# A planned kernel whose order is now the best of six schedules, with two buffers for v and r and one for S

## The chip, the core and the metric

The kernel runs on one core of a Trainium2 chip. The core has five engines that run side by side, each with its own queue of instructions that it takes strictly in order: PE (TensorE, matmuls), DVE (VectorE), ACT (ScalarE), POOL (GpSimd) and SP (SyncE, which here issues nearly all DMAs). [...] The metric is the device time of one execution in microseconds (us), as the median of several runs; less is better.

## The reference

Three stages follow each other. The first is a recurrence over 768 time steps for 4 batches x 8 heads with a 40x40 state each; the second and third are feed-forward blocks on 3072 tokens of width 320.

```python
for t in range(S):                                   # S = 768, state: (4, 8, 40, 40)
    y[:, :, t] = np.einsum('bhd,bhde->bhe', rt, state)
    Sa = np.einsum('bhde,bhe->bhd', state, at)
    state_decay = state * wt[:, :, None, :] - np.einsum('bhd,bhe->bhde', Sa, bt)
    state = state_decay + np.einsum('bhd,bhe->bhde', vt, kt)
...
h = x @ w_in                                         # 320 -> 2048, "Moe1"
g = h * np.tanh(np.log1p(np.exp(np.minimum(h, 20.0))))   # h itself where h > 20
x = g @ w_out                                        # 2048 -> 320
...
gate = 1.0 / (1.0 + np.exp(-(x @ w_gate)))           # 320 -> 1536, "Moe2"
return (gate * (x @ w_val)) @ w_out                  # 1536 -> 320
```

## The kernel before

**The recurrence ("attention").** The 768 steps are cut into 12 windows of 64. In a window each of the 4 batches is a unit, so there are 48 units; two units make a pair. For a unit, `load` brings `PA` (decays and a) and `KB` (k and b), `load2` brings `R` and `V` (r and v), `scale` forms decay products on DVE, `natural` (PE L441) transposes k and b. For a pair, `gram` (PE L423) forms the products of k, b and a. For a window, `solve` inverts a triangular system: 30 short DVE steps (`stmp`, L41, and `X`, L46, by turns) on 16x16 blocks, a round trip through DRAM, and for each of the two pairs four PE products (L564, L572, L581, L592/593). Then per unit or pair: `rv` (PE L459, r times v, reads `R` and `V`), `proj` (PE L622, r times the state `S` that the same batch had a window earlier; it reads `R` and `S`), `rhs` (PE L642 and L648), `zed` (PE L673), `close` (PE L706, then DVE L710), and `state` (PE L739, a transpose of the new state, which ACT copies to `S` at L743). `proj` is the last reader of its unit's `R`.

**The feed-forward blocks.** Moe1 takes a window's 256 tokens as soon as its four units are closed: 16 PE products into `ph` (L933, 8 matmuls of 128x256 each), ACT and DVE for the nonlinearity in groups of four (Sigmoid L976, Arctan L984, Sin L987, and a product on DVE, L41), a split in a high and a low part (`hi`, `lo`), and PE products into `x` (L1010 to L1023; L1007 opens a window's accumulation). Moe2 (PE L933 into `pgv`, L1137 to L1139) starts when all of the attention and nearly all of Moe1 are done, since its weights take over the attention's memory. Weights arrive as 64-bit numbers and are decoded on the core by DVE instructions in fours (L784, L786, L788, L794): Moe1's at the start, Moe2's ("parked" in DRAM) through the whole first part.

**What sets the order.** No order is written by hand. Every operation is recorded in a `Plan` with its engine (or a choice of engines), its planned duration, what it reads and writes, and a priority (`prio`, an early or late due time that its caller computes from constants such as `L` and `LA`). `Plan.order` then simulates the engines: step by step it takes, of the operations that could start within a few hundredths of a microsecond, the one of smallest priority, and so fixes for each engine the order in which its instructions are issued. On PE a rule beside the priorities steers the mix of attention and feed-forward products (`ratio`, `debt`, `DENSE`). The planned durations of DVE and ACT operations get `EACH` on top (0.08 and 0.09 us).

**Buffers.** `Attention.RINGS` gives the number of buffers of each kind of tile. A tile may be written when every reader of the tile that had its buffer before is done; the planner counts with that (`alloc`), and the semaphores of the built program enforce it. `R` and `V` have one buffer each: the DMAs of the next unit's r and v wait for the `proj` of the unit before.

Of the kernel before, what the change touches and what calls it, by code (L numbers as in the profile page):

```python
# [15 lines left out]
B, H, S, D = 4, 8, 768, 40  # L16
# [39 lines left out]
SEM = {('PE', 'PE'): 0.0, ('PE', 'DVE'): .32, ('PE', 'Act'): .32, ('Act', 'PE'): .37, ('DVE', 'PE'): .37, ('Pool', 'PE'): .37, ('SP', None): 0.0}  # L56
# [4 lines left out]
WAIT, URGENT = .09, 60.0  # L61
TICK, WARM = 3.413, 3060
TABLE = 1.283
EACH = {'DVE': .08, 'Act': .09}
SWITCH = .16
BIAS = {'PE': 0.0, 'DVE': 0.0, 'Act': 0.0, 'Pool': 0.0, 'SP': 0.0}
WIN = {'PE': .06, 'DVE': .06, 'Act': .06, 'Pool': .06, 'SP': .06}


class Op:  # L70
    __slots__ = ('eng', 'dur', 'lat', 'fn', 'alloc', 'prio', 'kind', 'need', 'out', 'ready', 'end', 'tiles', 'id', 'port')


class Plan:
# [7 lines left out]
    def __init__(s, rings, now=False):  # L82
        s.rings, s.now = rings, now
        s.ops, s.last, s.reads, s.users = [], {}, {}, {}
        s.n = 0

    def op(s, eng, dur, r, w, fn, alloc=(), prio=0.0, kind=None, lat=0.0, port=True):
        if s.now:
# [3 lines left out]
        if isinstance(eng, dict):  # L92
            eng = {e: d + EACH.get(e, 0.0) for e, d in eng.items()}
        elif eng in EACH:
            dur += EACH[eng]
        o.eng, o.dur, o.lat, o.fn, o.alloc, o.prio, o.kind = eng, dur, lat, fn, alloc, prio, kind
# [25 lines left out]
        return s.n  # L122

    def order(s, ratio):
        free = {}
        ready = {}

        def release(o):
            for e in o.eng if isinstance(o.eng, dict) else (o.eng,):
                ready.setdefault(e, []).append(o)  # L130

        for o in s.ops:
            for d in o.need:
                d.out.append(o)
            o.need = len(o.need)
            if not o.need:
                release(o)
        rings = {t: [None] * n for t, n in s.rings.items()}
        count = {t: 0 for t in rings}
        done, past, fetched = [], [], []  # L140
        debt = dma = acc = 0.0
        tick = 0
        warm = False
        table = last = None
        att = sum(o.kind == 'att' for o in s.ops)

        ports = {}

        def port(o, e):
            return ports.get('Pool' if e == 'DVE' else 'DVE', 0.0) if o.port and e in ('DVE', 'Pool') else 0.0  # L150

        def start(o, e):
            t = max(free.get(e, 0.0), port(o, e))
            if e == 'Act' and o.kind and o.kind != table:
                t += TABLE
            t = max(o.ready, t)
            if o.kind == 'bulk':
                t = max(t, dma - BACK)
            if o.kind == 'fetch' and len(fetched) >= 8:
                t = max(t, fetched[-8])  # L160
            if isinstance(o.eng, dict):
                b = BIAS if att else {}
                end = t + o.eng[e] + b.get(e, 0.0)
                if any(max(o.ready, free.get(x, 0.0), port(o, x)) + d + b.get(x, 0.0) < end for x, d in o.eng.items() if x != e):
                    return None
            used = {}
            for k in o.alloc:
                c = count[k[0]] + used.get(k[0], 0)
                used[k[0]] = used.get(k[0], 0) + 1
                old = rings[k[0]][c % len(rings[k[0]])]  # L170
                for u in s.users.get(old, ()):
                    if u.end is None:
                        return None
                    t = max(t, u.end + SEM.get((u.eng, e), .27))
            return t

        while len(done) < len(s.ops):
            best = None
            for e, l in ready.items():
                c = [(t, o) for t, o in ((start(o, e), o) for o in l) if t is not None]  # L180
                if not c:
                    continue
                m = min(t for t, o in c)
                late = [(o.prio, o.id, t, o) for t, o in c if m + WIN.get(e, 0.0) < t <= m + (FIRST if o.kind == 'first' else WAIT)]
                c = [(o.prio, o.id, t, o) for t, o in c if t <= m + WIN.get(e, 0.0)]
                if late and e != 'PE':
                    top = min(late, key=lambda x: x[:2])
                    if top[0] + URGENT < min(c, key=lambda x: x[:2])[0]:
                        c = [top]
                if e == 'PE' and ratio:  # L190
                    want = 'moe' if debt < 0 else 'att'
                    while past and past[0][0] < m - TICK:
                        past.pop(0)
                    if sum(x for _, x in past) < DENSE:
                        want = 'moe'
                    p = [x for x in c if x[3].kind == want]
                    c = p or c
                p = min(c, key=lambda x: x[:2])
                if best is None or p[2] < best[0]:
                    best = p[2], p[3], e  # L200
            assert best, "no operation can go next"
            t, o, e = best
            if isinstance(o.eng, dict):
                for x in o.eng:
                    ready[x].remove(o)
                o.dur, o.fn = o.eng[e], lambda f=o.fn, e=e: f(e)
                o.eng = e
            else:
                ready[e].remove(o)
            for k in o.alloc:  # L210
                g = rings[k[0]]
                g[count[k[0]] % len(g)] = k
                count[k[0]] += 1
            if e == 'SP':
                x = t
                for issue, kb in o.dur:
                    x += issue
                    dma = max(x + .65, dma) + kb / 360
                free['SP'], o.end = x, dma
            elif o.kind == 'fetch':  # L220
                free[e] = t + .1
                dma = max(t + 1.5, dma) + o.dur / 360
                o.end = dma + .8
                fetched.append(o.end)
            elif e == 'PE':
                x, left, work = t + (SWITCH if last and o.kind != last else 0.0), o.dur, o.lat or 2400 * o.dur
                last = o.kind
                while tick < int(x / TICK):
                    warm, acc, tick = acc >= WARM, 0.0, tick + 1
                while left > 1e-9:  # L230
                    rate = 1.0 if warm else .5
                    d = min(left / rate, (tick + 1) * TICK - x)
                    acc += work * d * rate / o.dur
                    left -= d * rate
                    x += d
                    if left > 1e-9:
                        warm, acc, tick = acc >= WARM, 0.0, tick + 1
                past.append((x, work))
                free['PE'] = o.end = x
                debt += o.dur if o.kind == 'moe' else -ratio * o.dur  # L240
                debt = max(-3.0, min(3.0, debt))
                if o.kind != 'moe':
                    att -= 1
            else:
                o.end = t + o.dur + o.lat
                if e is not None:
                    free[e] = t + o.dur
                if o.port and e in ('DVE', 'Pool'):
                    ports[e] = t + o.dur
                if e == 'Act' and o.kind:  # L250
                    table = o.kind
            done.append((t, len(done), o))
            for d in o.out:
                d.need -= 1
                d.ready = max(d.ready, o.end + (.32 if isinstance(d.eng, dict) else SEM.get((o.eng, d.eng), .27)))
                if not d.need:
                    release(d)
        s.span = max(o.end for o in s.ops)
        s.trace = done
        return [o.fn for _, _, o in done]  # L260


class Attention:
# [10 lines left out]

    RINGS = {'bk': 3, 'PA': 8, 'KB': 3, 'R': 1, 'V': 1, 'Kn': 6, 'E': 1, 'P64': 8, 'Gk': 3, 'Gb': 1, 'GS': 1, 'X': 1, 'U': 1, 'XT': 2, 'Q': 1,
             'stmp': 1, 'rs': 2, 'S': 2, 'xo': 1, 'vz': 2, 'gd': 2, 'xd': 2}

    def __init__(s, nc, plan, pool, dpool, banks, ins):  # L280
        s.nc, s.plan, s.p, s.dp, s.banks = nc, plan, pool, dpool, banks
# [20 lines left out]
    def tile(s, shape, tag):  # L302
        return s.p.tile(shape, F32, name=tag, tag=tag, bufs=s.RINGS[tag])

# [769 lines left out]
class Moe2:  # L1074
# [26 lines left out]
    def block(s, w, src, need, dst, at, then=lambda: None):  # L1101
# [51 lines left out]
        for f in range(NF2 + lag):  # L1153
# [16 lines left out]
RINGS = {**Attention.RINGS, 'hs': 2, 'tmp': 2, 'hi': 2, 'lo': 2, 'X6': 1, 'raw': 1, 'X7': 2, 'ph': 3, 'px': 1, 'dw': 1, 'dx': 1, 'raw2': 2,  # L1170
         'pgv': 3, 'g2': 2, 'g2h': 3, 'g2l': 3, 'y': 1}
# [292 lines left out]
```

## Time and profile before

| what | value |
|---|---|
| median of 3 runs | 1297.1 us (1292.1 to 1299.68) |
| the profiled execution | 1298.93 us, its span 1297.2 us |
| PE busy | 1159.2 us, 89% of the span |
| DVE busy | 860.7 us, 66% |
| ACT busy | 578.7 us, 45% |
| mean granted clock of PE | 0.94 |

The profile is of one execution. Its span runs from the first to the last instruction; what lies outside is 1.7 us. Busy times are sums over an engine's instructions without overlaps. [...] In a list of waits a row names the waiting engine and line, and behind the arrow what came last of that for which it waited.

### The profile page before, as it was taken

To read this page: it belongs to the slowest core of one execution; us is meant where nothing else is said; L and a number is where in the kernel's file an instruction comes from. 1 tells how busy PE (TensorE), PEld (TensorE's weight loads), DVE (VectorE), ACT (ScalarE), POOL (GpSimd) and SP (SyncE) were. 2 spreads that over 40 slices of the span, in tenths; PEclk is the share of its full clock that TensorE was granted. 3 is DMA by queue.
4 is the path that set the end of the run, shared out by engine and by line. 5 is a ranking of instruction groups with operands and counts; after the bars stand their busy time and mean duration, and the time that the engine had idled before them with its cause. 6 is when DMAs were issued, how large, how long until landed. Compare 5 with 4: busy or idle time off the path is not lost. (4 is left out here: it accounts for less than half of the span.)

```text
span 1297.2 us, 43316 instructions
## 1 busy us (share of the span) xinstructions
PE 1159.2 (89%) x18540; PEld 1093.2 (84%) x18540; DVE 860.7 (66%) x2238; ACT 578.7 (45%) x1061; POOL 126.4 (10%) x188
## 2 busy tenths in 40 slices
PE   4277759989999999988989798989999999999997
PEld 4266648888988888978878797989999999999997
DVE  7878888858787777768777677765844444444443
ACT  3134535656766576846547374774211111111111
POOL 2010110111011101010112100122100000000000
PEclk9997658989999899989979698989999999999999
DMA  8545463445353536445444434349500000000000
GB/s 242 150 133 135 101 173 86 123 111 134 102 143 97 152 98 154 101 97 142 119 116 124 120 85 112 80 111 369 166 24 23 23 24 23 24 24 11 11 11 14
DMA packets 205388, 132.47 MB, mean 102 GB/s; under 512 B 113537, under 2 KB 183554, under 8 KB 204802
## 3 DMA queue, kind: packets, MB, share of 16 engines
q1 hardware_dynamic: 196882, 117.80, 34.6%
q0 software_dynamic: 8304, 11.80, 3.8%
q8 instruction: 148, 2.42, 0.8%
q14 instruction: 54, 0.44, 0.1%
HBM read 98.08 MB, written 31.46 MB: 100 GB/s over the span
## 5 line engine op out<-in xcount | busy, mean ns | idle before, releaser
L933 PE MATMUL pgv<-X,w2in 128*128 128x256 f32 x2304 | 295.8, 281 | 0.0
L933 PEld LDWEIGHTS pgv<-X,w2in 128*128 128x128 f32 x2304 | 286.3, 188 | 0.0
L933 PE MATMUL ph<-X,win 128*128 128x256 f32 x1536 | 222.2, 295 | 5.9 <-ACT tmp L976 3.3
L933 PEld LDWEIGHTS ph<-X,win 128*128 128x128 f32 x1536 | 202.3, 199 | 10.9 <-ACT tmp L976 3.5
L1116 ACT ACTIVATE g<-pgv 128x256 f32<-128x256 f32 x144 | 55.4, 385 | 316.6 <-PE pgv L933 315.3
L1119 DVE TENSOR_TENSOR g<-pgv,g 128x256 f32<-128x256 f32 x144 | 60.9, 424 | 187.0 <-ACT g L1116 187.0
L1010 PE MATMUL x<-hi,wout 128*128 128x256 f32 x384 | 110.2, 308 | 6.6 <-DVE hi L51 4.0
L1011 PE MATMUL x<-hi,wout 128*128 128x256 f32 x384 | 103.5, 290 | 0.0
L1020 PE MATMUL x<-lo,wout 128*128 128x256 f32 x384 | 86.2, 307 | 0.7 <-DVE lo L46 0.7
L1010 PEld LDWEIGHTS x<-hi,wout 128*128 128x128 f32 x384 | 75.9, 198 | 11.8 <-DVE hi L51 4.3
L459 PE MATMUL at<-R,V 40*64 40x64 f32 x768 | 39.9, 255 | 43.2 <-DMA V<-vt 40.6
L1011 PEld LDWEIGHTS x<-hi,wout 128*128 128x128 f32 x384 | 76.3, 199 | 0.6
L459 PEld LDWEIGHTS at<-R,V 40*64 40x64 f32 x768 | 34.0, 164 | 49.8 <-issue 19.8
L41 DVE TENSOR_TENSOR hs<-hs,tmp 128x1024 f32<-128x1024 f32 x48 | 58.2, 1219 | 18.7 <-ACT tmp L987 18.5
L976 ACT ACTIVATE tmp<-ph 128x512 f32<-128x512 f32 x96 | 56.3, 597 | 30.4 <-PE ph L933 27.9
L1020 PEld LDWEIGHTS x<-lo,wout 128*128 128x128 f32 x384 | 61.1, 197 | 5.3 <-DVE lo L46 0.9
L46 DVE TENSOR_TENSOR g2l<-g,g2h 128x256 fp32r<-128x256 f32 x139 | 58.8, 424 | 4.0 <-ACT g2h L53 0.2
L466 DVE TENSOR_TENSOR VZ<-at,cst 64x256 f32<-64x256 f32 x96 | 40.3, 419 | 26.5 <-PE at L459 25.7
L987 ACT ACT_TABLE_LOAD x44 | 56.5, 1283 | 0.7
L976 ACT ACT_TABLE_LOAD x44 | 56.5, 1283 | 0.6
L46 DVE TENSOR_TENSOR lo<-hs,hi 128x512 fp32r<-128x512 f32 x82 | 54.7, 684 | 2.6 <-ACT hi L53 2.1
L987 ACT ACTIVATE tmp<-tmp,half 128x1024 f32<-128x1024 f32 x48 | 54.9, 1150 | 0.5
(177 smaller groups left out, 2389.8 us busy)
## 6 DMA issues: line engine op xcount, KB each, us to landing
PA<-pa SPq DMA_DIRECT2D x48, 260.0 KB
KB<-kb SPq DMA_DIRECT2D x48, 256.0 KB
dw<-w2in SPq DMA_DIRECT2D x30, 256.0 KB
w2in<-wd POOLq DMA_DIRECT2D x12, 640.0 KB, 14.7
R<-rt SPq DMA_DIRECT2D x48, 128.0 KB
V<-vt SPq DMA_DIRECT2D x48, 128.0 KB
gd<-Gb SPq DMA_DIRECT2D x48, 128.0 KB
wd<-dx SPq DMA_DIRECT2D x24, 256.0 KB
```

The source lines that it names most:

```text
L41: (nc.vector if e == 'DVE' else nc.gpsimd).tensor_tensor(out=out, in0=x, in1=y, op=ALU.mult)
L46: (nc.vector if e == 'DVE' else nc.gpsimd).tensor_tensor(out=out, in0=y, in1=x, op=ALU.subtract)
L459: nc.tensor.matmul(ps[64 * q:64 * q + 64, x:x + 64], d['V'][r, p, :], d['R'][r, p, :], start=True, stop=True)
L466: nc.vector.tensor_tensor(out=out, in0=ps[r, 0:256].rearrange("p (r a t) -> p r a t", r=2, a=2), in1=m, op=ALU.mult)
L933: nc.tensor.matmul(ps, W[:, a, c:c + 128], X[:, b, :], start=(i == 0), stop=(i == len(pairs) - 1))
L976: nc.scalar.activation(st['q', f // 4][:, f % 4 - 1:f % 4 + 1], st['ph', f // 2], AF.Sigmoid, scale=-1.0)
L987: nc.scalar.activation(st['q', g], st['q', g], AF.Sin, scale=-2.0, bias=s.half)
L1010: nc.tensor.matmul(p, O[:, 128 * j:128 * j + 128], hi, start=False, stop=False)
L1011: nc.tensor.matmul(p, O[:, 384 + 128 * j:512 + 128 * j], hi, start=False, stop=False)
L1020: nc.tensor.matmul(s.px[0][:, 256 * j:256 * j + 256], O[:, 128 * j:128 * j + 128], lo, start=False, stop=z and j == 1)
L1116: nc.scalar.activation(st['g', f], st['p', f][:, 0], AF.Sigmoid)
L1119: nc.vector.tensor_tensor(out=st['g', f], in0=st['p', f][:, 1], in1=st['g', f], op=ALU.mult)
```

## The change

`Plan.order` no longer schedules once. It makes six schedules. The first uses the callers' priorities and the PE rule as before. After each, `latest` walks the schedule backwards and computes for every operation the latest time at which it may start without lengthening that schedule (through its readers, the next operation on its engine, and the next user of its buffer); this time plus half of the caller's priority is the operation's priority in the next schedule. From the second on the PE rule is off (`ratio` 0). The schedule with the shortest planned span is kept. `EACH` is empty now, so planned durations of DVE and ACT are those written at each operation. `R` and `V` get two buffers each, `S` one instead of two. No operation is added or removed; where an operation has a choice of engines (DVE, ACT or POOL), the new schedule may choose otherwise.

```diff
@@ -61,14 +61,15 @@
-EACH = {'DVE': .08, 'Act': .09}
+PASSES, MIXED, PULL = 6, 1, 0.5
+EACH = {}
...
     def order(s, ratio):
+
+        best = None
+        for o in s.ops:
+            o.pred, o.list, o.aim = frozenset(o.need), o.eng, o.prio
+        for i in range(PASSES):
+            got = s.schedule(ratio if i < MIXED else 0)
+            s.log.append(s.span)
+            if best is None or s.span < best[0]:
+                best = s.span, [(t, k, o, o.eng) for t, k, o in got]
+            if i < PASSES - 1:
+                s.latest(got)
...
+    def latest(s, got):
+
+        late = {o: s.span - (o.end - t) for t, _, o in got}
...
+        for t, _, o in reversed(got):
+            x = late[o]
+            for d, lag in after[o]:
+                x = min(x, late[d] - (min(at[d] - t, o.took) if lag is None else o.end - t + lag))
+            late[o] = x
+        for o in s.ops:
+            o.prio = late[o] + PULL * o.aim
+
+    def schedule(s, ratio):
...
-    RINGS = {'bk': 3, 'PA': 8, 'KB': 3, 'R': 1, 'V': 1, 'Kn': 6, 'E': 1, 'P64': 8, 'Gk': 3, 'Gb': 1, 'GS': 1, 'X': 1, 'U': 1, 'XT': 2, 'Q': 1,
-             'stmp': 1, 'rs': 2, 'S': 2, 'xo': 1, 'vz': 2, 'gd': 2, 'xd': 2}
+    RINGS = {'bk': 3, 'PA': 8, 'KB': 3, 'R': 2, 'V': 2, 'Kn': 6, 'E': 1, 'P64': 8, 'Gk': 3, 'Gb': 1, 'GS': 1, 'X': 1, 'U': 1, 'XT': 2, 'Q': 1,
+             'stmp': 1, 'rs': 2, 'S': 1, 'xo': 1, 'vz': 2, 'gd': 2, 'xd': 2}
```

The diff puts 50 lines ahead of the attention's code, so what is L459 before is L509 in the changed kernel.

On PE, in the tenth window (units 36 to 39, batches 0 to 3), before: two closes (L706), two transposes of k and b (L441), the states of units 34 and 35 (L739), `proj` (L622) of unit 38, `rv` (L459) of unit 38, and the start of `gram` (L423).

```order
L706 MATMUL at_104<-VZ_113,Kn 40x104 x8
L706 MATMUL at_102<-VZ_113,Kn 40x104 x8
L441 MATMUL at_103<-cst,KB 128x104 x4
L441 MATMUL at_104<-cst,KB 128x104 x4
L739 MATMUL at_102<-cst,SU_110 40x40 x8
L739 MATMUL at_103<-cst,SU_111 40x40 x8
L622 MATMUL at_104<-R,S 40x64 x8
L459 MATMUL at_102<-R,V 64x64 x8
L423 MATMUL at_103<-PA,KB 64x64
```

The `rv` of unit 39 (the next L459) stands behind the rest of that gram alone, and its `R` and `V` may be loaded only after the L622 shown. In the changed kernel, the same place: a close's last transpose, Moe1 products, then both `rv` at once.

```order
L491 MATMUL at_103<-cst,KB 128x104 x4
L1070 MATMUL x_0_130<-lo,wout 128x256 x2
L1071 MATMUL x_1_131<-lo,wout 64x256
L1073 MATMUL x_1_131<-hi,wout 128x256
L983 MATMUL ph<-X_9790,win 128x256 x24
L509 MATMUL at_104<-R,V 64x64 x8
L509 MATMUL at_102<-R,V 64x64 x8
L983 MATMUL ph<-X_9790,win 128x256 x8
L789 MATMUL at_103<-cst,SU_110 40x40 x8
L1057 MATMUL x_0_130<-hi,zero 128x512
```

The `rv` of units 38 and 39 (L509) now stand side by side ahead of the `proj` (L672) of either, with a Moe1 product (L983) and a state (L789) behind them; the `proj` of units 38 and 39 come later, with a gram and Moe1 work between.

On DVE, in the first window's solve, before: the steps (`stmp`, `X`) follow each other with one `Gk` ahead.

```order
L46 TENSOR_TENSOR X<-X,stmp 128x8x8
L41 TENSOR_TENSOR stmp<-X,GS 128x63
L46 TENSOR_TENSOR X<-X,stmp 128x9x7
L41 TENSOR_TENSOR stmp<-X,GS 128x60
L46 TENSOR_TENSOR X<-X,stmp 128x10x6
L41 TENSOR_TENSOR stmp<-X,GS 128x55
L46 TENSOR_TENSOR X<-X,stmp 128x11x5
L41 TENSOR_TENSOR stmp<-X,GS 128x48
L46 TENSOR_TENSOR X<-X,stmp 128x12x4
```

In the changed kernel, the same steps, by turns with the decoding of Moe1's first weights (`hs`, `hi`, L836 to L844).

```order
L41 TENSOR_TENSOR stmp<-X,GS 128x63
L836 SCALAR_TENSOR_TENSOR hs<-hs 128x256
L46 TENSOR_TENSOR X<-X,stmp 128x9x7
L476 TENSOR_TENSOR Gk<-at_103,cst 128x512
L41 TENSOR_TENSOR stmp<-X,GS 128x60
L838 SCALAR_TENSOR_TENSOR hi<-hi 128x256
L46 TENSOR_TENSOR X<-X,stmp 128x10x6
L838 SCALAR_TENSOR_TENSOR hs<-hs 128x256
L41 TENSOR_TENSOR stmp<-X,GS 128x55
L844 SCALAR_TENSOR_TENSOR hi<-hi 128x256
L46 TENSOR_TENSOR X<-X,stmp 128x11x5
L844 SCALAR_TENSOR_TENSOR hs<-hs 128x256
```

So the decoding moved from behind the first solve into it.

## Rows read from the trace of the kernel before

**Rows 1.** A table by stage; busy time and count of each engine, granted clock, DMA share, GB/s

```profile
core 0: us, PE busy (x) PEld busy (x) DVE busy (x) ACT busy (x) POOL busy (x), PEclk, DMA share, GB/s
0.00:53.00 53.00, 18.88 (x376) 16.29 (x376) 40.67 (x122) 12.50 (x32) 7.07 (x17) 1.00 0.76 203
53.00:198.00 145.00, 96.47 (x2306) 85.31 (x2308) 120.34 (x383) 58.82 (x132) 15.18 (x25) 0.77 0.51 135
198.00:251.00 53.00, 51.88 (x1000) 47.20 (x997) 44.73 (x118) 32.97 (x62) 7.92 (x12) 0.96 0.42 110
251.00:871.00 620.00, 573.39 (x11547) 526.62 (x11547) 453.03 (x1139) 389.58 (x645) 77.97 (x113) 0.93 0.45 115
871.00:897.00 26.00, 25.32 (x212) 25.07 (x211) 13.29 (x22) 17.94 (x23) 12.72 (x16) 1.00 1.49 347
897.00:1297.00 400.00, 393.29 (x3113) 392.76 (x3112) 188.62 (x458) 66.91 (x171) 5.53 (x6) 1.00 0.14 41
```

**Rows 2.** L1007, which opens each Moe1 window's accumulation: least, median and longest ns, first and last start

```profile
L1007 PE MATMUL x<-hi,zero x12: 395/493/795, 198.5 to 871.0; 128*128 128x512 f32 x12
```

**Rows 3.** PE's waits, 251 to 871 us: total, times, longest

```profile
PE at L459 <- DMA V<-vt: 28.0, 15, 3.8
```

**Rows 4.** PE's waits, 53 to 198 us

```profile
PE at L564 <- DVE GS L558: 23.3, 2, 14.3
PE at L459 <- DMA V<-vt: 5.5, 3, 2.9
```

**Rows 5.** PE in order of time, units 38 and 39: start, duration, instructions, idle before

```profile
652.24 0.50 PE L739 MATMUL at<-cst,SU 40*40 40x40 f32 x16 [0.33 <-ACT S L743]
652.54 0.65 PE L622 MATMUL at<-R,S 40*40 40x64 f32 x16
652.99 0.93 PE L459 MATMUL at<-R,V 40*64 40x64 f32 x16
653.65 1.98 PE L423 MATMUL at<-PA,KB 40*64 40x64 f32 x64
658.52 0.98 PE L459 MATMUL at<-R,V 40*64 40x64 f32 x13 [2.88 <-DMA V<-vt]
```

**Rows 6.** The chain that ended last, at the same place: start, duration

```profile
653.95 0.36 SPq L351
...
654.35 4.04 DMA V<-vt
```

**Rows 7.** A stretch with such a wait (columns as in Rows 1)

```profile
650.00:660.00 10.00, 6.20 (x170) 5.62 (x171) 6.76 (x23) 2.56 (x7) 2.49 (x4) 0.66 0.54 130
```

**Rows 8.** PE in order of time: 13 Moe1 products back to back

```profile
858.49 12.63 PE L933 MATMUL ph<-X,win 128*128 128x256 f32 x104
```

**Rows 9.** DVE in order of time: two decodings side by side

```profile
46.48 0.42 DVE L786 SCALAR_TENSOR_TENSOR tmp<-tmp 128x256 int32<-128x256 int32 x1
46.81 0.42 DVE L788 SCALAR_TENSOR_TENSOR hs<-hs 128x256 int32<-128x256 int32 x1
```

**Rows 10.** Groups by line and form: operations that change engines, S, Sin and its table

```profile
L41 DVE TENSOR_TENSOR KB<-KB,E 128x512 f32<-128x512 f32 x29 | 21.8, 752 | 5.2 <-DMA KB<-kb 5.2
L51 DVE COPY hs<-ph 128x512 f32<-128x512 f32 x39 | 26.9, 690 | 33.4 <-ACT tmp L976 24.4 <-PE ph L933 8.4
L51 DVE CAST hi<-hs 128x1024 fp32r<-128x1024 f32 x22 | 15.2, 693 | 0.4
L743 ACT ACTIVATE S<-at 104x160 f32<-104x160 f32 x44 | 13.3, 302 | 13.4 <-PE at L739 12.4 <-DVE X L46 0.6
L987 ACT ACTIVATE tmp<-tmp,half 128x1024 f32<-128x1024 f32 x48 | 54.9, 1150 | 0.5
L987 ACT ACT_TABLE_LOAD x44 | 56.5, 1283 | 0.7
```

More of the change, by code (lines that the diff above doesn't have):

```diff
@@ L70 @@
 class Op:
-    __slots__ = ('eng', 'dur', 'lat', 'fn', 'alloc', 'prio', 'kind', 'need', 'out', 'ready', 'end', 'tiles', 'id', 'port')
+    __slots__ = ('eng', 'dur', 'lat', 'fn', 'alloc', 'prio', 'kind', 'need', 'out', 'ready', 'end', 'tiles', 'id', 'port', 'pred', 'list', 'aim', 'took')
 class Plan:
@@ L85, in __init__ @@
         s.n = 0
+        s.log = []
     def op(s, eng, dur, r, w, fn, alloc=(), prio=0.0, kind=None, lat=0.0, port=True):
@@ L124, in order @@
     def order(s, ratio):
+        best = None
[8 more added lines that the diff above has]
+                s.latest(got)
+        s.span = best[0]
+        for _, _, o, e in best[1]:
+            o.eng = e
+        s.trace = [x[:3] for x in best[1]]
+        return [(lambda f=o.fn, e=e: f(e)) if isinstance(o.list, dict) else o.fn for _, _, o, e in best[1]]
+    def latest(s, got):
+        late = {o: s.span - (o.end - t) for t, _, o in got}
+        after, rings, count = {}, {t: [None] * n for t, n in s.rings.items()}, {t: 0 for t in s.rings}
+        last = {}
+        for t, _, o in got:
+            a = after[o] = []
+            for d in o.pred:
+                after[d].append((o, SEM.get((d.eng, o.eng), .27)))
+            if o.eng is not None and o.eng in last:
+                after[last[o.eng]].append((o, None))
+            last[o.eng] = o
+            for k in o.alloc:
+                g, c = rings[k[0]], count[k[0]]
+                for u in s.users.get(g[c % len(g)], ()):
+                    if u is not o:
+                        after[u].append((o, SEM.get((u.eng, o.eng), .27)))
+                g[c % len(g)] = k
+                count[k[0]] = c + 1
+        at = {o: t for t, _, o in got}
+        for t, _, o in reversed(got):
[6 more added lines that the diff above has]
+    def schedule(s, ratio):
         free = {}
@@ L132, in order @@
         for o in s.ops:
-            for d in o.need:
+            o.eng, o.out, o.ready, o.end = o.list, [], 0.0, None
+            o.need = len(o.pred)
+        for o in s.ops:
+            for d in o.pred:
                 d.out.append(o)
-            o.need = len(o.need)
             if not o.need:
@@ L205, in order @@
                     ready[x].remove(o)
-                o.dur, o.fn = o.eng[e], lambda f=o.fn, e=e: f(e)
+                o.dur = o.eng[e]
                 o.eng = e
@@ L251, in order @@
                     table = o.kind
+            o.took = free.get(e, t) - t if e is not None else 0.0
             done.append((t, len(done), o))
@@ L258, in order @@
         s.span = max(o.end for o in s.ops)
-        s.trace = done
-        return [o.fn for _, _, o in done]
+        return done
 class Attention:
-    RINGS = {'bk': 3, 'PA': 8, 'KB': 3, 'R': 1, 'V': 1, 'Kn': 6, 'E': 1, 'P64': 8, 'Gk': 3, 'Gb': 1, 'GS': 1, 'X': 1, 'U': 1, 'XT': 2, 'Q': 1,
-             'stmp': 1, 'rs': 2, 'S': 2, 'xo': 1, 'vz': 2, 'gd': 2, 'xd': 2}
+    RINGS = {'bk': 3, 'PA': 8, 'KB': 3, 'R': 2, 'V': 2, 'Kn': 6, 'E': 1, 'P64': 8, 'Gk': 3, 'Gb': 1, 'GS': 1, 'X': 1, 'U': 1, 'XT': 2, 'Q': 1,
+             'stmp': 1, 'rs': 2, 'S': 1, 'xo': 1, 'vz': 2, 'gd': 2, 'xd': 2}
     def __init__(s, nc, plan, pool, dpool, banks, ins):
```

## The prediction, made before the changed kernel ran

> **What bounds the kernel now.** I read the table by stage first [rows 1]. The reader is to see where PE stands still. From 897 us to the end PE is busy 393 of 400 us at full clock: Moe2, a wall of matmuls whose order the change leaves as it is; the hand-over to it (871 to 897 us) has PE busy 25.3 of 26 us. From 251 to 871 us (attention and Moe1 mixed) PE is busy 573.4 of 620 us, so 46.6 us are idle, and the granted clock is 0.93 instead of 1.00, which costs at most 573.4 x 0.07 = 40 us more. From 53 to 198 us PE is busy only 96.5 of 145 us at clock 0.77, and DVE is the busiest engine, 120.3 us or 83%: that stage waits for the solves and for weights that DVE decodes. Before it (0 to 53 us) PE waits mostly for the first window's data and solve, 18.9 of 53 us busy; behind it (198 to 251 us) PE is full, 51.9 of 53. The last start of L1007, at 871.0 [rows 2], ends the mixed part. Everything before it that shortens PE's path shortens the kernel one for one, since PE does the same work afterwards.
>
> Then I read who keeps PE waiting. In the mixed part one cause stands out: `rv` waits for the DMA of `V`, 15 times, 28.0 us, so 60% of the 46.6 us idle [rows 3]. In the stage before, the largest is the solve (23.3 us), and `V` is 5.5 us [rows 4].
>
> **Part 1: two buffers for R and V.** One place shows the mechanism. `proj` of unit 38 (L622) starts at 652.54; only when it has read `R` may the next `R` be issued, at 653.95, then `V` at 654.35, which takes 4.04 us to land [rows 5, 6]. PE has only a gram (1.98 us) to put between, and stands idle 2.88 us before the next `rv`. From the L622's start to that L459's it is 6.0 us. With two buffers the transfer waits for the `proj` of two units earlier, and the new order puts both `rv` of a pair side by side, ahead of both `proj`. Between the releasing `proj` and the `rv` that needs the transfer now stand Moe1 products, states and a gram. I weighed the rows of the order with durations from the steady part (a Moe1 product of 8 matmuls is 12.63/13 = 0.97 us [rows 8], and so on by line). This estimate gives a median of 3.8 us of work between the two before, and 19 us with a least of 5.5 us now. The need is the 6.0 us from start to start less the 0.65 us of `proj`, so about 5.3 us. All 15 waits should go: -28.0 us, with a bound of 0 on the other side if something else is late at the same place. Next late there would be the states and `rhs`; the row with 0.33 us behind `ACT S` [rows 5] is the size I expect.
>
> **Part 2: the clock.** The wait stands in a stretch of 10 us with PE busy 6.2 us and clock 0.66 [rows 7]. The mixed part loses up to 40 us to the clock [rows 1]. If the loss follows the idle time, 60% of it, 24 us, belongs to the `V` waits. But these stretches also hold small attention matmuls, which stay. I take 20 us given back, with bounds 0 and 40.
>
> [...]
>
> **Part 3: one buffer for S.** `S` of a unit may be written when the `proj` of the one before has read it, and each `proj` waits for its own `S`, so 44 trips PE, ACT, PE become serial. The copy takes 0.302 us [rows 10]; a state that follows another waits 0.33 us for it [rows 5]. By the same weighing the new order has a median of 2.2 us of PE work between a state and its `proj` (7.3 before), a least of 0.8. That mostly covers it. I take +3 us; the bounds are 0 and 44 x 1.2 = 53 (half of a table load and a Sin, 1.283 + 1.150 [rows 10], that ACT may have to finish first).
>
> **Part 4: the order at the start.** Counted over the new order, 167 instead of 124 decoding instructions (L784 to L794) stand ahead of the eighth L710 on DVE, which closes the second window. Neighbours start 0.33 us apart though each shows 0.42 us [rows 9], so 43 of them are 14 us of DVE. With DVE at 83% the second window closes up to 17 us later. In exchange the last decoding of Moe1's weights comes after 470 instead of 510 DVE instructions, and the first L1007 stands ahead of 13 attention products that preceded it. I expect PE to lose time until the second window closes and to regain it when Moe1 is dense earlier: 0, with bounds -10 and +17.
>
> **Part 5: planned times without a margin, other engines.** The two neighbours in [rows 9] also show that `EACH` counted 0.08 us too much per DVE operation: 0.33 is the planned 0.34. The new plan has DVE about right. The choices move 17 products on `KB` from POOL to DVE (17 x 0.752 = +12.8 us), 25 copies of `hs` away from DVE (-17.3) and 11 casts of `hi` to it (+7.6) [rows 10]: +3 us on DVE, which is 73% busy in the mixed part [rows 1], hidden by PE. ACT gets two more pairs of table loads, 5 us, also hidden: it is 63% busy there. If PE's idle time shrinks, DVE comes to some 78%, still no bound. A denser plan without margins makes new small waits; PE's idle time beside `V` is 46.6 - 28.0 = 18.6 us. I take +5; the bounds are 0 and 18.6 (as much again).
>
> **The sum.** The profiled execution took 1298.9 us (span 1297.2 and 1.7 around it). 1298.9 - 28 - 20 + 3 + 0 + 5 = 1258.9. It lay 1.8 us above the median of 1297.1, so the forecast for the median is 1257 us.
>
> **Rivals.**
> A. The whole cold clock comes back with the waits: -28 - 40 + 3 = -65, so 1232. For it: wait and low clock stand together [rows 5, 7]. Against: from 53 to 198 us the clock is 0.77 although `V` costs only 5.5 us there [rows 1, 4], so small attention products lower it too.
> B. The start slips and stays late: +17 on the main sum, 1274. For it: DVE is the busiest engine there, and 49 more DVE instructions stand ahead of the second window's close. Against: the weights come earlier, and the third window's close stands behind nearly as many as before (580 against 582).
> C. No change: the `V` waits only move to the next product on the chain (`rhs` waiting for `SU`, `zed` for the solve), 1297. For it: attention is a long chain. Against: the new order draws Moe1 products between its links, and a window has (871.0 - 198.5)/11 = 61 us [rows 2] in which to pass the chain once.
> D. Slower: the single `S`. If each of the 44 trips meets ACT in the middle of a Sin, Arctan or table load, and PE, in order, stands for 1.2 us at the `proj`, that is 53 us, 50 more than the 3 taken: 1307. It decides against the change from about 0.95 us per trip on. For it: ACT has 44 table loads and 48 Sin activations of L987 alone [rows 10], and the distance shrank from 7.3 to 2.2 us. Against: in the new order nine of the 44 copies come right behind one of Moe1's Sigmoid, Arctan or Sin (eleven before).
>
> **Chances.** The main case, 1257 with its own range 1244 to 1268: 0.48. A 0.15, B 0.17, C 0.08, D 0.12. For this kernel 0.5% (6.5 us) is about what a measurement tells from no change. Main, A and B are faster by more: 0.80. C is the same: 0.08. D is slower: 0.12. The range from 1232 to 1300 takes in A, B and C and leaves out most of D.
>
> **What would show it.** Right: the row PE at L459 behind DMA `V` falls from 28 us to under 3 in the mixed part; the last start of L1007 comes near 831 instead of 871.0; the clock there rises from 0.93 to about 0.96; the first L1007 stays within 10 us of 198.5; PE's waits behind ACT `S` stay under 5 us. Wrong: `V` gone but the last L1007 later than 860, with a new name in the waits; PE at `proj` behind ACT `S` with tens of us (D); the first L1007 beyond 210 (B). The stage after the last L1007 must stay at 426 us within 5; if it doesn't, I have overlooked something in the hand-over to Moe2.

## The result, and the profile after

The changed kernel takes 1258.7 us (median of four runs, 1254.3 to 1266.8) against 1296.4 of the kernel before in the same session: a ratio of 0.972, interval 0.965 to 0.979. The forecast was 1257. The profiled execution is the longest of the four and has the lowest clock (0.958; the others 0.965 and 0.966): 1266.8 us with a span of 1265.0, so 32.2 us shorter than the one before.

The table by stage, cut at the same marks as [rows 1] (first, second and last opening of a Moe1 window); `PEclk` is the granted clock of PE as the profile records it, a share of full speed, in the mean of the stretch:

```profile
core 0: us, PE busy (x) PEld busy (x) DVE busy (x) ACT busy (x) POOL busy (x), PEclk, DMA share, GB/s
0.00:53.00 53.00, 20.24 (x376) 16.77 (x376) 40.82 (x125) 13.33 (x33) 5.94 (x16) 1.00 0.75 213
53.00:174.00 121.00, 82.65 (x1869) 72.70 (x1870) 108.68 (x339) 55.02 (x133) 15.31 (x24) 0.82 0.53 142
174.00:231.00 57.00, 52.35 (x1228) 48.25 (x1228) 43.63 (x107) 38.04 (x67) 7.30 (x12) 0.97 0.47 120
231.00:836.00 605.00, 566.09 (x11726) 521.13 (x11724) 460.25 (x1171) 398.44 (x666) 82.03 (x118) 0.95 0.49 127
836.00:863.00 27.00, 26.07 (x218) 25.67 (x217) 14.97 (x22) 20.00 (x25) 1.96 (x4) 1.00 1.22 308
863.00:1265.00 402.00, 395.41 (x3132) 395.14 (x3131) 188.42 (x462) 66.32 (x169) 6.24 (x7) 0.99 0.09 30
```

The openings themselves, to be held against [rows 2]:

```profile
L1057 PE MATMUL x<-hi,zero x12: 395/484/501, 173.9 to 836.1; 128*128 128x512 f32 x12
```

The reader is to see where the 32.2 us come from. The second opening moved from 251 to 231: 20 us are won before the stage on which the forecast put all of its gain. The mixed part is 605 instead of 620 us: 15 us, where 40 were forecast (28 + 20 - 3 - 5). The stage behind it is 2.7 us longer (428.9 for 426.2). Over the whole span PE is idle 122.2 us instead of 138.0 and busy 1142.8 us instead of 1159.2 with the same 18540 matmuls: half of the gain is less waiting, half is less time for the same products, beside a higher clock (0.958 for 0.940).

PE's waits from 231 to 836 us, longest first, against [rows 3]:

```profile
PE at L672 <- DVE VZ L516: 5.9, 3, 3.3
PE at L756 <- DVE VZ L735: 5.6, 3, 2.6
PE at L614 <- DVE GS L608: 4.2, 4, 2.1
PE at L614 <- issue: 2.8, 1, 2.8
PE at L491 <- ACT S L793: 2.0, 2, 1.8
```

The row of `rv` behind the DMA of `V` is gone, all 28.0 us of it. But PE's idle time there is 605 - 566.1 = 38.9 us, before 46.6. So 20 of the 28 us came back as many small waits on DVE and ACT. The clock rose from 0.93 to 0.95; the loss to it, an estimate from busy time and clock as in the prediction, fell from 40 to 566.1 x 0.05 = 28 us.

PE at the place of [rows 5] in the changed kernel (start, duration):

```profile
619.16 1.15 PE L509 MATMUL at<-R,V 40*64 40x64 f32 x32
620.24 1.22 PE L983 MATMUL ph<-X,win 128*128 128x256 f32 x8
621.39 0.50 PE L789 MATMUL at<-cst,SU 40*40 40x40 f32 x16
621.82 0.49 PE L1057 MATMUL x<-hi,zero 128*128 128x512 f32 x1
...
624.54 0.62 PE L672 MATMUL at<-R,S 40*40 40x64 f32 x16
```

Both `rv` of the pair run in one piece (32 matmuls), with no wait ahead, and the `proj` follow later. Locally the change does what the prediction said.

In the stage of [rows 4] the long wait stays, with another name behind the arrow:

```profile
PE at L614 <- ACT win L53: 21.4, 1, 21.4
```

It is a product of the first window's solve, which reads `GS` and `U`; ACT's copy of a decoded weight (`win`) is merely what ended last by the profile. The product itself starts at 58.77 us, before at 53.53; in the new order decodings stand between the steps of this solve.

DVE between 53 and 100 us, before and then after (columns as in the table by stage):

```profile
53.00:100.00 47.00, 31.24 (x832) 26.91 (x832) 37.96 (x122) 14.41 (x42) 6.71 (x11) 1.00 0.50 139
```

```profile
53.00:100.00 47.00, 25.70 (x700) 22.22 (x702) 44.02 (x133) 18.98 (x52) 6.82 (x11) 1.00 0.55 145
```

DVE is busy 44.0 of 47 us instead of 38.0, and PE does less. From 0 to the first opening DVE stands idle 37.0 us before (198.5 less 161.5 busy) and 24.5 us after (173.9 less 149.4). That is the second thing to see, and the prediction had no term for it. It is half of the 24.6 us by which the first opening comes sooner; the other half is 12.1 us of DVE work that the new order puts behind the opening.

### The profile page after: what moved, and what is told of

Its sections match the earlier page's. It is cut to its first block, busy times and chain, and to the rows that moved or that the text cites. A ratio compares the mean times of both kernels' runs of the same rounds, so it can differ in the third digit from the quotient of the medians.

```text
span 1265.0 us, 43282 instructions
## 1 busy us (share of the span) xinstructions
PE 1142.8 (90%) x18540; PEld 1079.7 (85%) x18540; DVE 856.8 (68%) x2221; ACT 591.1 (47%) x1091; POOL 118.8 (9%) x179
## 4 chain that ended last, share of the span: by engine, by line
PE 47%; SPq 4%; DVE 3%; DMA 3%; issue 1%; ACT 1%; DVEq 0%; ACTq 0%
PE pgv L983 22%; PE ph L983 5%; PE ph L1187 2%; PE x L1187 2%; PE x L1189 2%; PE ph L1189 2%; PE x L1188 2%; PE ph L1188 2%; PE x L1060 1%; PE x L1070 1%; SPq L538 1%; PE at L756 1%; PE x L1061 1%; SPq L588 1%; PE x L1071 1%
## 5 line engine op out<-in xcount | busy, mean ns | idle before, releaser
L983 PE MATMUL pgv<-X,w2in 128*128 128x256 f32 x2304 | 296.0, 281 | 0.0
L983 PEld LDWEIGHTS pgv<-X,w2in 128*128 128x128 f32 x2304 | 286.4, 188 | 0.1
L983 PE MATMUL ph<-X,win 128*128 128x256 f32 x1536 | 229.2, 297 | 1.6 <-ACT X L53 1.1
L983 PEld LDWEIGHTS ph<-X,win 128*128 128x128 f32 x1536 | 205.9, 201 | 6.7 <-issue 1.5
L1070 PE MATMUL x<-lo,wout 128*128 128x256 f32 x384 | 83.5, 300 | 0.5 <-DVE lo L46 0.5
L53 ACT ACTIVATE hs<-ph 128x512 f32<-128x512 f32 x82 | 48.4, 594 | 45.3 <-PE ph L983 43.3
L756 PE MATMUL at<-VZ,Kn 128*40 128x104 f32 x768 | 51.7, 287 | 14.6 <-DVE VZ L735 9.2
L1026 ACT ACTIVATE tmp<-ph 128x512 f32<-128x512 f32 x96 | 56.6, 596 | 8.5 <-PE ph L983 6.7
L46 DVE TENSOR_TENSOR lo<-hs,hi 128x512 fp32r<-128x512 f32 x85 | 58.5, 702 | 1.3 <-ACT hi L53 0.5
L756 PEld LDWEIGHTS at<-VZ,Kn 128*40 128x40 f32 x768 | 41.8, 134 | 20.3 <-DVE VZ L735 8.6
L41 DVE TENSOR_TENSOR stmp<-X,GS 128x15 f32<-128x15 f32 (+4 forms) x180 | 41.4, 230 | 23.9 <-DMA GS<-gd 14.8
```

What stands on the lines that cost most here:

```text
L41: (nc.vector if e == 'DVE' else nc.gpsimd).tensor_tensor(out=out, in0=x, in1=y, op=ALU.mult)
L46: (nc.vector if e == 'DVE' else nc.gpsimd).tensor_tensor(out=out, in0=y, in1=x, op=ALU.subtract)
L756: nc.tensor.matmul(ps[64 * q:64 * q + 40, p, :], d['Kn'][:, 2 * p + q, :], s.VZ[k % 2][:, q, p % 2, 2 * (u % 2) + p // 2, :], start=True, ...
L983: nc.tensor.matmul(ps, W[:, a, c:c + 128], X[:, b, :], start=(i == 0), stop=(i == len(pairs) - 1))
L1026: nc.scalar.activation(st['q', f // 4][:, f % 4 - 1:f % 4 + 1], st['ph', f // 2], AF.Sigmoid, scale=-1.0)
L1070: nc.tensor.matmul(s.px[0][:, 256 * j:256 * j + 256], O[:, 128 * j:128 * j + 128], lo, start=False, stop=z and j == 1)
```

## The experiments

The change has three parts that can be made alone: the buffers (`R` and `V` two, `S` one), the six schedules, and the margin `EACH` dropped. With the two ends known, six kernels fill the table of all eight combinations. Two more ask what the buffers do when the order stays as it was, and four look into the margin and the schedules. All ratios are against the kernel before on the same chip.

**The buffers without a new order.** The two kernels keep the order of before word for word; only memory has a second buffer of one of the two tiles.

```diff
-        return s.p.tile(shape, F32, name=tag, tag=tag, bufs=s.RINGS[tag])
+        return s.p.tile(shape, F32, name=tag, tag=tag, bufs={'V': 2}.get(tag, s.RINGS[tag]))
```

> The kernel before, word for word in its order, with two buffers of V in memory (its planner still counts one). Theory 1 (the buffers give the gain): all 15 long waits of TensorE for V's transfer go, 28 us, and part of the cold clock behind them: 1255 to 1272 us. Theory 2 (the new order of the start and of the end gives most of it): the waits go too, but the instructions behind them stand where a planner that counted one buffer put them, so much of the time is waited for elsewhere; by the middle of the changed kernel, which is only about 5 us nearer to its work than that of before, 1278 to 1292 us. Theory 3 (V was only where TensorE happened to wait): 1293 to 1300 us, with new waits of about 28 us in the mixed part.

Measured: ratio 0.998, 0.995 to 1.001; no change. My theories 1 and 2 both expected the waits to go, and that was wrong. PE's wait from 251 to 868 us, and the queue of SP at the place of [rows 5, 6] (start, time to issue):

```profile
PE at L459 <- DMA V<-vt: 25.7, 12, 3.3
```

```profile
655.63 0.36 SPq L351 DMA_DIRECT2D R<-rt  x1
656.03 0.43 SPq L352 DMA_DIRECT2D V<-vt  x1
```

SP issues `R` ahead of `V`, and `R` still waits for the products that read it: `proj` ran from 654.48 to 655.13 and `rv`, which reads `R` too, from 654.94 to 655.60. `V` stands behind it in the queue. So the next kernel has `{'R': 2}` in the same line instead.

> The kernel before in its own order, with two buffers of R in memory and one of V. With two of V alone the waits for V stayed, so the reason now tested is the queue: SyncE issues R's transfer first, which waits for proj to have read R, and V's stands behind it. Theory 5 (R's buffer holds V's transfer back): the waits for V fall from about 34 us in all to under 8, and the loss between the first and the last start of the accumulation falls by 15 to 23 us: 1275 to 1286 us. Theory 6 (the order behind is made for the old buffers): waits for V go, but others take their place: 1292 to 1300 us. If V's transfer is late for its own sake, the row stays above 20 us and the time at 1294 to 1303.

Measured: 0.998, 0.995 to 1.000, again nothing. The rows of the same places:

```profile
PE at L459 <- DMA V<-vt: 25.4, 12, 4.8
```

```profile
653.09 0.36 SPq L331 DMA_DIRECT2D PA<-pa  x1
653.49 0.44 SPq L351 DMA_DIRECT2D R<-rt  x1
654.04 0.37 SPq L352 DMA_DIRECT2D V<-vt  x1
```

Here `R` no longer waits for `proj` (652.80 to 653.45); it is issued 0.04 us after the issue of `PA` ahead of it has ended, and `V` 0.11 us after that of `R`. So it is at every wait of PE for `V` in this kernel's mixed part: `R` is issued 0.04 to 0.06 us after the issue ahead of it, `V` 0.05 to 0.11 us after `R`. Neither buffer holds the transfer there for longer than that. In the old order the issues of `R` and `V` stand behind others in SP's queue, here behind that of `PA`, which ends at 653.45. The expectation "late for its own sake" had the right numbers, but the cause is the place in the queue.

The kernel before shows the same at eight of its 15 waits for `V` (16.6 of the 28.0 us): `R` is issued at most 0.12 us after the issue ahead of it, with its last reader done earlier. One of them is the longest wait of [rows 3], 3.76 us ahead of the `rv` at 571.65. The last `proj` before it had ended at 563.77; SP's queue there (start, time to issue):

```profile
559.99 4.79 SPq L488 DMA_DIRECT2D GS<-gd  x8
564.82 0.45 SPq L331 DMA_DIRECT2D PA<-pa  x1
565.37 0.38 SPq L858 DMA_DIRECT2D wd<-dx  x1
565.85 0.42 SPq L351 DMA_DIRECT2D R<-rt  x1
566.32 2.62 SPq L352 DMA_DIRECT2D V<-vt  x1
```

At the other seven SP does wait for a product that reads `R`. In the old order either buffer alone buys nothing. Both together in the old order were not tried; the rows of this run leave them little to win. The next kernel gives both to a planner that counts with them and may issue them earlier.

**The eight combinations.** The expectations call the margin "spacings". Their theories are: 1, the buffers give the gain; 2, the order from the latest times does; 4, dropping the margin does. The edits are single lines of the changed kernel put back, or, for the margin alone, one taken over:

```diff
-PASSES, MIXED, PULL = 6, 1, 0.5
+PASSES, MIXED, PULL = 1, 1, 0.5
-EACH = {}
+EACH = {'DVE': .08, 'Act': .09}
-    RINGS = {... 'R': 2, 'V': 2, ... 'S': 1, ...}
+    RINGS = {... 'R': 1, 'V': 1, ... 'S': 2, ...}
```

New buffers, one schedule, old margin:

> The changed kernel with one schedule instead of six and the old spacings: the planner of before with the new buffers alone. Theory 1 (buffers): 1255 to 1268 us, no wait for V. Theory 2 (order of start and end, from the latest times): no wait for V either, but the first accumulation still opens after 190 us and the last stage of the mixed part still loses time: 1280 to 1294 us.

New buffers, one schedule, no margin:

> The changed kernel with one schedule instead of six; new buffers and new spacings. Beside the kernel with the old spacings too it gives what the spacings are worth under one schedule. Theory 2 (latest times matter): 1278 to 1294 us, within 6 us of the run with old spacings. Theory 4 (spacings): 1255 to 1266 us, over 15 us below the run with old spacings. Theory 1 (buffers): both runs at 1255 to 1268 us.

Old buffers, six schedules, no margin:

> The changed kernel with the buffers of before (one of R and V, two of S); six schedules and the new spacings stay. Theory 1 (buffers): near the time before, 1285 to 1297 us, with the waits for V back. Theory 2 (order of start and end): keeps the early first accumulation and the full last stage of the mixed part, about 24 of the 38 us: 1264 to 1276 us. Theory 4 (the spacings): as the changed kernel, 1255 to 1265 us.

Old buffers, one schedule, no margin:

> The kernel before with the new spacings alone (EACH empty): one schedule, old buffers. Theory 4 (true durations on DVE and ACT give an order that closes the first windows sooner): the first accumulation opens near 185 us instead of 198.5, the waits for V stay at 25 to 40 us, 1272 to 1286 us. Rival (the spacings help only together with the new buffers): opens after 195 us, 1291 to 1303 us.

New buffers, six schedules, old margin:

> The changed kernel with the old spacings: six schedules and new buffers. Theory 4 (the spacings close the first windows sooner): the first accumulation opens after 190 us, 1278 to 1290 us. Theory 2 (the latest times do): opens by 180 us, 1256 to 1270 us.

Old buffers, six schedules, old margin:

> Six schedules alone, with the old buffers and the old spacings. Theory 4 (spacings): opens after 190 us, 1288 to 1301 us. Theory 2 (latest times): opens by 182 us, 1270 to 1282 us; with all waits for V at 20 to 40 us in both.

Measured. The openings are the first and last start of the line that opens a Moe1 window; "decodings" counts the instructions that decode weights which start on DVE before the fourth L710 (L760 in kernels with the changed planner; the first window's close); "DVE idle" is its idle time from 0 to the first opening.

| margin | schedules | buffers | ratio, interval | first, last opening | decodings | DVE idle, us |
|---|---|---|---|---|---|---|
| old | one | old | 1 | 198.5, 871.0 | 58 | 37.0 |
| old | one | new | 0.992, 0.990 to 0.995 | 203.7, 855.3 | 63 | 38.7 |
| old | six | old | 0.986, 0.981 to 0.991 | 202.7, 854.1 | 75 | 39.2 |
| old | six | new | 0.985, 0.981 to 0.990 | 204.2, 855.7 | 80 | 44.9 |
| none | one | old | 0.980, 0.977 to 0.983 | 189.4, 853.8 | 77 | 25.0 |
| none | one | new | 0.974, 0.969 to 0.978 | 185.6, 844.0 | 77 | 20.9 |
| none | six | old | 0.979, 0.974 to 0.984 | 179.1, 837.9 | 97 | 18.7 |
| none | six | new | 0.972, 0.965 to 0.979 | 173.9, 836.1 | 94 | 24.5 |

What follows. Dropping the margin is the largest part: 2.0% alone (26 us of 1297), and still 1.4% (18 us) when the other two are there, where the intervals do not meet. The buffers give 0.8% alone (10 us) and 0.7% on top of the rest; the six schedules give 1.4% alone and 0.2% on top of the rest; these last two steps lie inside the intervals. Alone the three add up to 4.2%, together they give 2.8%: they overlap. The kernel with the old buffers, which still waits 13.4 us for `V` in the mixed part (14 times, 231 to 838 us), has three quarters of the gain. Theory 1 (the buffers) falls; theory 2 (latest times) named the right size for the old buffers with six schedules (1275 us), but missed where the margin goes and the schedules stay one (1270 us for 1278 to 1294) and where the margin stays with new buffers and six schedules (1282 us for 1256 to 1270).

Theory 4 (the margin) came nearest: its run alone (1276), its 23 us between the two runs with new buffers and one schedule, and its late opening with old margin all came as it said. It missed three times: without the new buffers the rest does not reach the changed kernel (1275 for 1255 to 1265), and the six schedules alone give 1282 us, below its 1288, although they open as late as it said (they won their time after the opening: 651.5 us from first to last opening, 672.5 before). And its reason, that the first windows close sooner, is wrong: the first window closes at 93.8 us before, at 99.1 with the margin alone dropped and at 103.3 in the changed kernel. What comes sooner is the decoding of Moe1's weights. The six schedules alone were also expected to keep 20 to 40 us of waits for `V`; they keep 17.5 of 40.6 in the whole run, with one buffer, which again says that the order decides on these waits.

The first opening tells the cases apart: 198.5 to 204.2 us in all four kernels with the margin, 173.9 to 189.4 in all four without. So does DVE's idle time. Not all of it is kept: with new buffers and six schedules the opening comes 30 us sooner without the margin, but from first to last opening the kernel then needs 662 us instead of 651.5.

The buffers alone, from first to last opening, before and with them (columns as in the table by stage):

```profile
198.50:871.00 672.50, 624.77 (x12528) 573.38 (x12525) 497.26 (x1255) 422.30 (x704) 85.90 (x125) 0.94 0.45 114
```

```profile
203.70:855.30 651.60, 607.29 (x12438) 558.01 (x12435) 498.64 (x1249) 417.03 (x698) 84.66 (x118) 0.97 0.45 115
```

All waits for `V` are gone, but PE is idle 44.3 us instead of 47.7. Of the 20.9 us won, 17.5 are busy time, with the clock at 0.97 instead of 0.94. This is not one profile's chance: the granted clock of the whole kernel is 0.954 in the mean of eight executions with the buffers alone (0.948 to 0.957) and 0.940 in that of eighteen of the kernel before (0.935 to 0.950). That the clock rose because the waits went is not shown: with the margin alone dropped, 27.2 of 40.6 us of waits for `V` remain in the whole run, and the clock is 0.957 to 0.963 in five executions.

Why the buffers alone brought less than the 15.7 us by which their last opening came sooner: they lost 11.7 us behind it (437.9 us after the last opening, 426.2 before). The kernel with new buffers, one schedule and old margin, PE's largest wait from 855 to 900 us, and the stretch with it:

```profile
PE pgv L983 <- DMA w2in<-wd: 5.7, 2, 3.5
```

```profile
875.00:895.00 20.00, 10.91 (x82) 10.07 (x80) 6.28 (x15) 4.18 (x8) 7.96 (x12) 0.98 1.34 349
```

In these 20 us PE is busy 10.9 while the DMAs, the loads of Moe2's weights among them, move 349 GB/s. In the other seven kernels of the table the stage takes 424 to 429 us. The first of these loads (`w2in` from `wd`) is issued at 871.8 us here, as late as before (870.9), though the last opening came at 855.3; in the six other kernels it is issued 1 to 19 us ahead of the last opening. So PE met a transfer that had been hidden.

**Which margin.** The changed kernel with one half of the old margin each:

```diff
-EACH = {}
+EACH = {'Act': .09}
```

> The changed kernel with the old margin on ACT alone (0.09 us per instruction), none on DVE. Theory 4a (the margin on DVE, the fullest engine until the first windows close, is what cost time): the first accumulation opens by 182 us and the time stays at 1256 to 1268 us. Theory 4b (ACT's margin): opens after 190 us, 1274 to 1288 us. If both count about evenly: 1266 to 1276 us in this run and the next.

And with `{'DVE': .08}`:

> The changed kernel with the old margin on DVE alone (0.08 us per instruction), none on ACT. Theory 4a: the first accumulation opens after 190 us, as with both margins, 1274 to 1288 us. Theory 4b: opens by 182 us, 1256 to 1268 us.

Measured: with ACT's margin 0.973 (0.968 to 0.978), as the changed kernel; with DVE's 0.985 (0.980 to 0.991), as with both. Theory 4a stands. Of all kernels here whose planner was changed, the four planned with DVE's margin measure 0.985 to 0.992 and the seven without it, the next two experiments among them, 0.970 to 0.980; so the gain is not that of one lucky order. The openings, and DVE from 53 to 100 us, first of the kernel with ACT's margin alone, then of that with DVE's:

```profile
L1057 PE MATMUL x<-hi,zero x12: 395/493/796, 169.4 to 829.2; 128*128 128x512 f32 x12
```

```profile
53.00:100.00 47.00, 23.85 (x680) 20.52 (x680) 45.78 (x142) 12.99 (x36) 7.61 (x12) 1.00 0.49 128
```

```profile
L1057 PE MATMUL x<-hi,zero x12: 395/494/793, 196.4 to 845.7; 128*128 128x512 f32 x12
```

```profile
53.00:100.00 47.00, 29.86 (x780) 25.83 (x784) 37.86 (x120) 18.07 (x51) 5.09 (x9) 0.85 0.52 138
```

DVE is busy 45.8 of 47 us in the one and 37.9 in the other, and 99 against 65 decodings come before the first window closes.

**Below the real spacing.** `EACH = {'DVE': -.02}` in the changed kernel:

> The changed kernel with every DVE instruction planned 0.02 us shorter still (0.32 us for a decoding instruction, which the trace spaces by 0.33). If what counts is that the planned spacing is the real one: no gain, 1255 to 1272 us. If a smaller number is simply better, since it draws DVE's work forward: 1238 to 1253 us, and the first accumulation opens before 170 us.

Measured: 0.974 (0.969 to 0.978), 1267 us. No gain, as expected of "the real spacing counts", although the first opening came earliest of all, at 166.4 us, with 111 decodings ahead of the first close. From first to last opening it needs 672 us (662 in the changed kernel). So an early opening is no end in itself.

**More schedules.** `PASSES` 24 for 6:

> The changed kernel with 24 schedules instead of six: another order that the planner holds to be as good as that of six. It tells how far two such orders lie apart on the chip. If further passes with latest times still help: below 1250 us. If they are used up and orders alike in plan are alike on the chip: 1254 to 1268 us. If order to order scatter is as large as what the buffers gave (0.7%): up to 1275 us.

Measured: 0.970 (0.965 to 0.974), 1263 us: another order, the same time. It opens at 186.4 and last at 831.1, and DVE's idle time before the first opening, 24.2 us, is that of the changed kernel. No version tried beats the changed kernel by more than the intervals.

## Why the forecast was right, and which steps were not

The sum came out (1257 for 1258.7), and its steps were wrong in opposite directions: in the profile the mixed part gave 15 us where 40 were forecast, and the stages ahead of it 20 where none were. That the number fits is luck.

- **Part 1, -28 us: the waits went, their time did not.** All waits for `V` went, but idle time in the mixed part fell by 7.7 us, and with the buffers alone by 3.4 us from first to last opening. The buffers alone measured 10 us, and 9 on top of the rest. The step that failed is that a wait removed is time won: the bound "0 if something else is late at the same place" was far nearer than the value taken, and next late were not "the states and `rhs`" alone but 23 rows of small waits, on `VZ`, `GS`, `X`, `rs`, `Q`. The mechanism, a transfer that waits for the reader of its buffer, holds at seven of the 15 places; at the other eight the issue stood in SP's queue behind others. And at the place shown [rows 5, 6] the reader that ended last was not `proj` (653.19) but `rv`, which reads `R` too (653.92; `R` was issued at 653.95).
- **Part 2, -20 us: 12 in the changed kernel, 19 with the buffers alone.** The clock in the mixed part rose from 0.93 to 0.95, not to 0.96; with the buffers alone the loss to the clock from first to last opening fell from 37 to 18 us (624.77 x 0.06 and 607.29 x 0.03). The size was about right, and with the buffers alone most of the time won there is busy time at the higher clock (17.5 of 20.9 us); both losses are estimates, and the link to the `V` waits is open, as said above. Part of it may be chance: the kernel before and the two old-order kernels, with the same order, show 0.94, 0.95 and 0.95 from first to last opening.
- **Part 3, +3 us: right.** PE's waits behind ACT `S` from 231 to 836 us are 2.7 us (L491 2.0, L509 0.7), none at `proj`.
- **Part 4, 0 us: wrong, some -20 by the second opening.** The counted shift was real: the second window closes 7 us later (173.7 for 166.7, where 14 to 17 were feared). But I let the early decoding merely repay this. It also lets Moe1 open 24.6 us sooner, half of it on DVE time that had been idle.
- **Part 5, +5 us: the wrong sign, and the heart of the change.** I read from [rows 9] that the margin counted 0.08 us too much per DVE operation, concluded that "the new plan has DVE about right", and then priced this as a loss of small waits. In the runs it is the largest gain. What the counts show is that without it more decodings stand between the instructions of the first windows' chain (94 for 58), and DVE waits less (24.5 us idle up to the first opening for 37.0). Why the planner does so is argued, not shown: an order made for a slower DVE has the decodings far behind the chain, and DVE then has less to do while the chain waits for PE or a DMA. The other counts of this part came as the order said:

```profile
L41 DVE TENSOR_TENSOR KB<-KB,E 128x512 f32<-128x512 f32 x46 | 31.2, 679 | 1.5 <-DMA KB<-kb 1.4
L51 DVE CAST hi<-hs 128x1024 fp32r<-128x1024 f32 x33 | 22.6, 683 | 1.6 <-PE x L1063 0.7
L51 DVE COPY hs<-ph 128x512 f32<-128x512 f32 x14 | 9.6, 687 | 15.0 <-PE ph L983 8.0 <-ACT tmp L1026 6.9
L1037 ACT ACT_TABLE_LOAD x46 | 59.0, 1283 | 0.8
```

  Against [rows 10]: 17 more products on `KB`, 25 fewer copies, 11 more casts, two more loads of this table and two of the other (L1026), all of it hidden; DVE is 76% busy in the mixed part.

**The rivals.** A (all of the loss to the clock comes back) is out: every wait for `V` is gone and the clock is 0.95, so by the same estimate 12 of 40 us came back and 28 are still lost to it. What keeps the rest is not shown; other small waits stand in place of those for `V`. That small attention products lower the clock, as said against A, was the author's inference: the stage from 53 to 198 us also holds 23.3 us of waits for the solve [rows 4], and no run tells the two apart. Its 0.77 is not sure either: the profile gives 1.00 from 80 to 100 us, where 16 matmuls of the same `rv` took 1.12 us at 88.45 and 0.68 at 99.15. B (the start slips) had the right place and the wrong sign. C (the waits only move) was given 0.08 and is most of the truth about PE's idle time: 20 of 28 us came back under other names. But it forecast no change, and the buffers alone still gave 10 us, with a higher clock. D (the single `S`) is out, at 2.7 us.

**The signs named.** `V`'s row under 3 us: yes, gone. Last opening near 831: 836.1. Clock near 0.96: 0.95. `S` under 5 us: yes. Stage behind 426 within 5: 428.9. First opening within 10 us of 198.5: no, 24.6 sooner; that one miss pointed at the failed steps.

## What to carry to other kernels

Where a planner fixes the order in which instructions are issued, its durations are part of the kernel: here a safety margin on the engine that is busiest in one stage went with more idle time of that engine on the chip (37.0 us for 25.0 with the margin alone dropped), and cost more than the waits that stand out in the list (26 us for the buffers' 10). Read a wait's row as the place where the time shows, not as its price: before a wait is booked as a gain, try it away with the order unchanged, look at PE's whole idle time, and see in the issuing engine's queue whether the transfer waited for a buffer or only for its turn. When several edits come at once, a table of all combinations says what a right total hides.

## What the runs showed that was not expected

- One order, one program, and yet another clock: the four executions of the changed kernel have mean granted clocks of 0.958, 0.965, 0.966 and 0.966, and spans of 1265.0, 1261.3, 1252.5 and 1252.5 us. At 1142.8 us of PE busy, 0.008 of clock is 9 us (an estimate) of the 12.5 between the ends; but the second, with nearly the clock of the last two, is 8.8 us longer than they, so the clock is not all of it. From 53 us to the first opening the order of before shows 0.77, 0.78 and 0.70 in three kernels that differ only in a buffer. A few us of clock in one profile are no evidence; the mean clocks of all executions are better.
- The same decoding of weights, 157 to 167 instructions, had started at the first opening in every kernel, wherever the opening fell between 166 and 204 us.
